# Chunk 3's second batch in natural row order, its tables built earlier, and one key load on another queue, in a fused attention and feed-forward kernel

## The chip, the cores and the metric

The kernel runs on one core of one Trainium2 chip. The metric is device time in microseconds (us) of one execution; lower is better. TensorE (PE) multiplies matrices, VectorE (DVE), ScalarE (ACT) and GpSimd (POOL) work on elements, and SyncE (SP) only issues transfers. GpSimd and ScalarE issue transfers too, each on a queue of its own.

## What is computed

Decayed linear attention in blocks of 64 rows, for 4 batches, 8 heads, 768 positions and 64 features, with a state handed from block to block, followed by a two-layer feed-forward step on all 3072 rows:

```python
Dmask = np.where(rel >= 0, lam[:, None, None] ** rel[None, :, :], 0.0)
lam_pow = lam[:, None, None] ** (pos[None, :, None] + 1)
lam_block = lam ** block
for b in range(nb):
    intra = np.einsum('bhic,bhjc->bhij', qb, kb) * Dmask[None]
    intra = np.einsum('bhij,bhjd->bhid', intra, vb)
    inter = np.einsum('bhid,bhde->bhie', qb * lam_pow[None], kv_state)
    out[:, :, sl] = intra + inter
    kb_dec = kb * rev_pow[None]
    kv_state = lam_block[None, :, None, None] * kv_state + np.einsum('bhsd,bhse->bhde', kb_dec, vb)
...
h = x @ w_in                      # x: 3072 x 512, w_in: 512 x 2048
g = np.maximum(h, 0.0) + alpha * np.minimum(h, 0.0)
return (g @ w_out).astype(np.float32)
```

## The kernel before

**Tiling.** A chunk is 512 rows: 256 positions (W) of two batches. There are six chunks, c = 0 to 5; chunk c covers positions c // 2 * 256 onward of batches 2 * (c % 2) and the next one. Within a chunk the work on attention goes in four units: batch bi (0 or 1) and half of the heads hh. Units are numbered 4c + 2 bi + hh, so units 14 and 15 are chunk 3, batch 1 (line 393).

**Two row orders.** For chunks below FIRST = 4 (line 75), a partition holds two neighbouring rows (`fetch`, lines 82 and 83), so that a load is one transfer with 512 B pieces, and the work goes in blocks of 128 positions (L). A unit then has a score matrix in pairs, two masks of 128 x 512 (`masked`, lines 617 to 627) and two states (`state`, `aged`, step L // N = 2 in `follows`). From chunk 4 on, a partition holds rows in their natural order: a load is two transfers with 256 B pieces (lines 85 and 86), the blocks have 64 positions (N), scores and outputs have half as many columns, a unit has one mask (line 642) and four states in a row, each of two scaled sums (L685). The second order has its own tables: nmask, nkdecay, nrdecay, nqdecay, built by `places_in_order` (five iotas on POOL, L320 to L322), `order_factors` (ACT, L325), `order_ahead` (DVE, L328), `order_mask_log` (two steps on POOL, L334 and L341), `order_query_log` (POOL, L346), `order_mask` (ACT, L354), `order_key_decay` (ACT, L357 and L358) and `order_query_decay` (ACT, L362).

**What happens to a unit.** k and q are loaded: k always as float32 on SyncE's queue (`load`, L100), q either so, or as float16 with the conversion in the transfer, on GpSimd's queue (`load16`, L110); v always the latter. `cast` (L398 ACT, L400 DVE, L402 POOL) makes float16 copies of what came as float32; `key_decayed` (L444, POOL) multiplies the keys by their decay; `turn` transposes k and q on TensorE (L466, L471), `turned` copies the result out of PSUM; `turn_by_dma` (L492) does the same by a transfer for units 12 and on. `decayed` (L508) makes the decayed queries. `cluster(old, new)` (L517 to L607) is the TensorE block that gives old its outputs and new its scores and state products. `out_of` copies the outputs to xT, from which the feed-forward step takes its rows.

**The feed-forward step.** `up` (L720: four products into one PSUM bank), `below` (ACT, L731), `gate` (DVE, L743), then `down` (L753: four products per part) and `store`. The bank of an up is free again when its gate has read it. bi None means both batches at once; in the first chunks it goes batch by batch.

**What sets the order.** Every engine runs its instructions in program order, and the program is written out by hand for chunks 0 and 1 and the attention of chunks 1 to 3 (lines 786 to 1175). From chunk 2 on a loop (lines 1255 to 1273) weaves the attention steps of chunk c + 1 evenly between the products of chunk c; in its first round the nine table builders are interleaved with the first nine attention steps (lines 1257 to 1269). GpSimd's queue is first in, first out: loads of w_in (`load_win`), w_out (`load_wout`), q and v as float16. `hold` (L97) writes one element of a tile early, so that the transfer into it has one thing to wait for.

Of the kernel before, what the change touches and what calls it, by code (L numbers as in the profile page):

```python
# [11 lines left out]
def kernel(  # L12
# [61 lines left out]
    N = 64  # L74
    FIRST = 4

    def fetch(queue, src, x, c, bi, part):

        h0, n = (0, H) if part is None else (part * H // 2, H // 2)
        pb, b = c // 2, 2 * (c % 2) + bi  # L80
        x, rows = x[:, ds(h0, n), :], src[b, ds(h0, n), ds(pb * W, W), :]
        if c < FIRST:
            queue.dma_start(out=x, in_=rows.rearrange("h (p e) d -> p h (e d)", e=2))  # L83
        else:
            for e in range(2):
                queue.dma_start(out=x[:, :, ts(e, D)], in_=rows[:, ts(e, L), :].rearrange("h p d -> p h d"))
# [11 lines left out]

    def load(x, c, bi, part=None):
        fetch(nc.sync, {"k": k, "q": q}[x], raw(x, c, bi), c, bi, part)  # L100

# [336 lines left out]
    def key_decayed(n, eng="G"):  # L438
        c, bi, hh = units[n]
        kr = view(raws[c, bi, "k"], hh)  # L440
        kdec = half_pool.tile([128, 2, 4, D], fp16, tag="kdec", name="kdec", bufs=4)
        for e in range(2):
            decay = kdecay[:, ds(4 * hh, 4), e] if c < FIRST else nkdecay[:, ds(4 * hh, 4)]
            engine(eng).tensor_tensor(  # L444
                out=kdec[:, e],
                in0=kr[:, e],
                in1=decay.unsqueeze(2).to_broadcast([128, 4, D]),
                op=ALU.mult,
            )
        T.setdefault(n, {})["kdec"] = kdec  # L450
# [47 lines left out]
    def decayed(n, eng="G"):  # L498
        c, bi, hh = units[n]
        t = T[n]  # L500
        qdT = qkt_pool.tile([128, 2, 2, L], fp16, tag="qdT", name="qdT")

        first = 1 if c // 2 == 0 else 0
        out, src = (
            y[:, :, :, ds(first * 64, L - first * 64)].rearrange("p e h (a j) -> p (e h) a j", j=64)
            for y in (qdT, t["qT"])
        )
        engine(eng).tensor_tensor(  # L508
            out=out,
            in0=src,  # L510
            in1=(qdecay if c < FIRST else nqdecay)[:, hh].rearrange("p e h j -> p (e h) j").unsqueeze(2).to_broadcast([128, 4, 2 - first, 64]),
            op=ALU.mult,
        )
        t["qdT"] = qdT
# [5 lines left out]
    def cluster(old, new, other=False):  # L520
# [3 lines left out]
        part = ot = acc = None  # L524
        if old is not None or units[new][0] < FIRST:
            acc = None if other else ps.tile([128, 2, 512], fp32, tag="acc", name="acc")
            part = [bank(a, "h_acc") if other else acc[:, a] for a in range(2)]
            ot = [x[:, 0:256].rearrange("p (h i) -> p h i", h=2) for x in part]
        if old is not None:
# [6 lines left out]
            def states(own):  # L536


                for e in range(1 if co < FIRST else 2):
                    for hl in range(2):  # L540
                        a = hl if own else 1 - hl
                        before = R.get((bb, ho, 4 * pbo + 2 * a if co < FIRST else 4 * pbo + 2 * e + a))
                        if before is None:
                            continue
                        for hp in range(2):
                            if co < FIRST:
# [14 lines left out]
            def outputs():  # L561
                nc.tensor.wait_ge(apart, waits[0])
                states(True)
                for hl in range(2):
                    for e in range(2):
                        for hp, a in QUADS:
                            p = ds(a * 64, 64)
                            if co < FIRST:
                                o, x = ot[a][ds(hp * 64, 64), hl, :], to["sm"][hl][p, hp, 1 - e, :]
                            else:  # L570
# [5 lines left out]
                                start=(2 * pbo + a == 0 and hl == 0 and e == 0),  # L576
                                stop=(e == 1 or co >= FIRST),
                                skip_group_check=True,
# [5 lines left out]
        if new is not None:  # L584
# [5 lines left out]
            for hp in range(2):  # L590
                for e in range(2):
                    for a, hl in QUADS:
                        p = ds(hl * 64, 64)
                        if c < FIRST:
                            o = sc[ds(a * 64, 64), hl].rearrange("p (h x e j) -> p h x e j", h=2, x=2, e=2)[:, hp, 1 - e]
# [6 lines left out]
                        )  # L602
        if old is not None and (new is None or c < FIRST):
            outputs()
        if new is not None:
            kv = t["kv"] = [
                (part[a] if c < FIRST else sc[:, a])[:, 256:512].rearrange("p (e h d) -> p e h d", e=2, h=2)  # L607
                for a in range(2)
            ]
            for hp in range(2):  # L610
                for e in range(2):
                    for hl in range(2):
                        for a in range(2):
                            if 4 * pb + 2 * e + a + 1 == S // N and c >= FIRST:
                                continue
                            p = ds(a * 64, 64)
                            nc.tensor.matmul(  # L617
                                kv[a][ds(hl * 64, 64), 0 if c < FIRST else e, hp, :],
                                lhsT=t["kdec"][p, e, hp + 2 * hl, :],
                                rhs=vn[p, e, hp + 2 * hl, :],  # L620
                                start=(c >= FIRST or old is None and hp == 0 and e == 0),
                                stop=(c >= FIRST or e == 1),
                                skip_group_check=True,
                            )
        if old is not None and not (new is None or c < FIRST):
            outputs()
# [37 lines left out]
    def follows(n, a):  # L664

        c, bi, hh = units[n]
        step = L // N if c < FIRST else 1
        b, i = 2 * (c % 2) + bi, 4 * (c // 2) + a * step
# [4 lines left out]
    def state(n, a):  # L673
# [8 lines left out]
        else:  # L682
            decay = rdecay if c < FIRST else nrdecay
            for hp in range(2):
# [76 lines left out]
    def store(c, t, c0=0, n=DM):  # L761
# [4 lines left out]
        rows = out[ds(b * S + pb * W, W), ds(c0, n)]  # L766
        rows = rows.rearrange("(j e) d -> e j d" if c < FIRST else "(e j) d -> e j d", e=2)[t // 2]
        nc.scalar.dma_start(out=rows, in_=o_sb[:, 0:n])
# [63 lines left out]
    cluster(None, 0)  # L832
    load_win(0, 256)
    mask_log(3)
# [4 lines left out]
    masked(0, 1)  # L839
    load_win(256, 256)  # L840
    fill(4)
# [46 lines left out]
    load("k", 1, 0)  # L888
    load("k", 1, 1)
    below(0, 1, 0)  # L890
# [50 lines left out]
    gate(0, 10, None)  # L941
    up(0, 12, None, 1)
    load16("v", 1, 1)
    key_decayed(4, "G")
# [8 lines left out]
    down(0, 2, 0, 0)  # L953
    load_wout(4, 4)
    turn(4)
# [112 lines left out]
    aged(12, 0)  # L1068
    aged(8, 1)
    gate(1, 1, 1)  # L1070
# [9 lines left out]
    up(1, 4, 1, 0)  # L1080
    out_of(8, "A")
    cast(11, "k", "G")
    masked(9, 0)
# [29 lines left out]
    gate(1, 6, None)  # L1113
    out_of(9, "A")
    cast(13, "q", "G")
    masked(10, 0)
# [82 lines left out]
    def in_order(x):  # L1199
        return units[x][0] >= FIRST  # L1200

# [53 lines left out]
    for c in range(2, NC):  # L1255
        att = attention_steps(c + 1) if c + 1 < NC else []
        if FIRST > 2 and c == 2:
            early = [
                places_in_order,
                order_factors,  # L1260
                order_ahead,
                lambda: order_mask_log(0),
                order_key_decay,
                lambda: order_mask_log(1),
                order_query_log,
                order_mask,
                order_query_decay,
            ]
            att = [y for z in zip(early, att) for y in z] + att[len(early) :]
        ups = [lambda f=f: up_whole(c, f) for f in range(NF)]  # L1270
# [35 lines left out]
```

## Time and profile before

| what | value |
|---|---|
| three runs | 217.02, 217.38, 218.69 us; median 217.38 |
| the profiled execution | 217.07 us; its span 215.3 |
| granted TensorE clock in it | 1.00 of full speed |
| busy: PE, weight loads, DVE, ACT, POOL | 206.1, 106.0, 123.0, 112.6, 97.4 us |
| instructions | 5683 |
| bytes | 27.28 MB read from HBM, 6.29 MB written |
| products of the feed-forward step, L720 and L753 | 96.7 and 81.2 us busy |

The span runs from the first instruction to the last; the 1.8 us around it belong to the execution but to no instruction. Busy times count instructions that compute; issuing a transfer is not counted. The page cuts the span into 40 slices and gives each engine's busy tenth in each. Below, "the chain" is the chain of work that ended last, "waits" are the idle times of an engine by what ended them, and "landing" is the moment at which a transfer's data are announced.

### The profile page before, as it was taken

How to read it: one execution, taken by the hardware profiler on the slowest of the kernel's cores; microseconds unless marked ns; L12 is line 12 of the kernel's file. 1: busy time of each engine (PE TensorE's matmuls, PEld its weight loads, DVE VectorE, ACT ScalarE, POOL GpSimd, SP SyncE). 2: the span in 40 equal slices, each digit the busy share in tenths (PEclk: the TensorE clock that was granted, in tenths of full speed). 3: DMA queues.
4: the chain of work that ended last, by engine and by line, in shares of the span. 5: the costliest groups of instructions: out<-in, count | busy, mean ns of one | idle time of the engine just before them, and what ended most of it. 6: DMA issues, size and time to landing. Idle time of an engine off the chain costs nothing.

```text
span 215.3 us, 5683 instructions
## 1 busy us (share of the span) xinstructions
PE 206.1 (96%) x2350; PEld 106.0 (49%) x2350; DVE 123.0 (57%) x259; ACT 112.6 (52%) x213; POOL 97.4 (45%) x155
## 2 busy tenths in 40 slices
PE   7978997899999999999999999999999999999993
PEld 2656543557665545454444444544444444444442
DVE  2787783849768785456576556756654344443000
ACT  5966665536656565465555555454444434443121
POOL 7899428867889561973895256422000000000000
PEclk9999999999999999999999999999999999999999
DMA  4999999999999494697689995313011101100212
GB/s 116 251 189 181 208 215 190 209 209 207 272 250 252 105 214 35 150 194 100 102 93 216 216 219 112 80 53 97 0 52 50 43 9 49 49 27 24 97 59 89
DMA packets 71194, 28.43 MB, mean 132 GB/s; under 512 B 52080, under 2 KB 68224, under 8 KB 71168
## 3 DMA queue, kind: packets, MB, share of 16 engines
q0 software_dynamic: 26592, 8.65, 35.9%
q1 hardware_dynamic: 40800, 13.11, 32.0%
q10 hardware_dynamic: 3776, 6.31, 8.1%
q8 instruction: 18, 0.29, 0.6%
q14 instruction: 8, 0.07, 0.1%
HBM read 27.28 MB, written 6.29 MB: 156 GB/s over the span
## 4 chain that ended last, share of the span: by engine, by line
PE 80%; DMA 7%; POOL 6%; ACT 3%; issue 1%; DVE 0%; ACTq 0%; POOLq 0%
PE h_ps L720 34%; PE o_ps L753 32%; DMA qh<-in_q_dram 7%; PE o_ps L775 6%; PE acc L552 3%; POOL kdec L444 2%; PE s L600 2%; PE acc L572 2%; POOL w_in_sb L116 2%; PE tp L471 1%; ACT qkT L398 1%; PE tp L466 1%; POOL qdT L508 1%; PE acc L617 1%; ACT L248 1%
## 5 line engine op out<-in xcount | busy, mean ns | idle before, releaser
L743 DVE SCALAR_TENSOR_TENSOR g<-m,oma,h_ps 128x512 f16<-128x512 f32 (+1 forms) x106 | 73.0, 696 | 64.1 <-ACT m L731 62.4
L720 PE MATMUL h_ps<-xT,w_in_sb 128*128 128x512 f16 (+1 forms) x424 | 96.7, 359 | 1.0 <-ACT R L679 0.6
L731 ACT ACTIVATE m<-h_ps 128x512 f32<-128x512 f32 (+1 forms) x106 | 59.0, 556 | 55.8 <-PE h_ps L720 53.9
L753 PE MATMUL o_ps<-w_out_sb,g 128*128 128x512 f16 x320 | 81.2, 379 | 0.0
L720 PEld LDWEIGHTS <-w_in_sb 128*128 128x128 f16 x424 | 39.6, 98 | 41.6 <-DMA w_in_sb<-in_moe_w_in_dram 1.1
L753 PEld LDWEIGHTS <-g 128*128 128x128 f16 x320 | 30.9, 98 | 35.8
L764 ACT ACTIVATE o_sb<-o_ps 128x512 f32<-128x512 f32 (+2 forms) x25 | 14.5, 579 | 18.8 <-PE o_ps L775 11.0
L444 POOL TENSOR_TENSOR kdec<-kraw,kdecay 128x256 f16<-128x256 f32 x32 | 19.5, 633 | 7.4 <-DMA kraw<-in_k_dram 6.6
L633 DVE TENSOR_TENSOR sm<-s,dmask 128x512 f16<-128x512 f32 x32 | 21.2, 684 | 2.8 <-PE s L600 2.7
L398 ACT ACTIVATE xT<-acc 128x512 f16<-128x512 f32 x22 | 13.1, 597 | 13.3 <-PE acc L572 9.0
L508 POOL TENSOR_TENSOR qdT<-qkT,nqdecay 128x512 f16<-128x512 f16 x8 | 9.3, 1164 | 18.9 <-DMA qkT<-qk 8.7
L701 POOL TENSOR_TENSOR old<-R,rdecay 128x128 f32<-128x128 f16 x21 | 8.3, 410 | 17.4 <-DVE R L681 14.8
L775 PE MATMUL o_ps<-w_out_sb,g 128*128 128x512 f16 (+2 forms) x80 | 14.0, 336 | 0.0
L508 POOL TENSOR_TENSOR qdT<-qkT,qdecay 128x512 f16<-128x512 f16 (+1 forms) x11 | 11.3, 1029 | 3.0 <-DVE qkT L400 1.9
L552 PE MATMUL acc<-qdT,R 64*64 64x64 f16 (+1 forms) x216 | 10.9, 217 | 0.2
L775 PEld LDWEIGHTS <-g 128*128 128x128 f16 x80 | 7.2, 98 | 6.9
L685 DVE SCALAR_TENSOR_TENSOR R<-R,nrdecay,s 128x64 f16<-128x64 f16 x48 | 10.5, 275 | 0.0
L552 PEld LDWEIGHTS <-R 64*64 64x64 f16 x224 | 5.9, 104 | 8.8 <-issue 5.9
L444 POOL TENSOR_TENSOR kdec<-kraw,nkdecay 128x256 f16<-128x256 f32 x16 | 9.5, 613 | 0.0
L572 PE MATMUL acc<-sm,vh 64*64 64x128 f16 (+1 forms) x352 | 8.5, 209 | 0.0
L83 POOL DMA_DIRECT2D vh<-in_v_dram x8 | 7.6, 945 | 0.8 <-POOLq L1290 0.8
L398 ACT ACTIVATE qk<-qraw 128x512 f16<-128x512 f32 x11 | 6.9, 624 | 2.0 <-DMA qraw<-in_q_dram 1.1
(107 smaller groups left out, 152.3 us busy)
## 6 DMA issues: line engine op xcount, KB each, us to landing
out_dram<-o_sb ACTq DMA_DIRECT2D x23, 256.0 KB, 2.3
kraw<-in_k_dram SPq DMA_DIRECT2D x12, 256.0 KB, 5.1
kraw<-in_k_dram SPq DMA_DIRECT2D x6, 512.0 KB, 11.4
qraw<-in_q_dram SPq DMA_DIRECT2D x10, 256.0 KB, 6.9
vh<-in_v_dram POOLq DMA_DIRECT2D x8, 256.0 KB, 10.5
w_out_sb<-in_moe_w_out_dram POOLq DMA_DIRECT2D x4, 512.0 KB, 9.4
w_in_sb<-in_moe_w_in_dram POOLq DMA_DIRECT2D x3, 512.0 KB, 6.7
qh<-in_q_dram POOLq DMA_DIRECT2D x5, 256.0 KB, 11.1
```

What stands on the lines that cost most here:

```text
L398: nc.scalar.activation(out, in_, AF.Copy)
L444: engine(eng).tensor_tensor(out=kdec[:, e], in0=kr[:, e], in1=decay.unsqueeze(2).to_broadcast([128, 4, D]), op=ALU.mult,)
L508: engine(eng).tensor_tensor(out=out, in0=src, in1=(qdecay if c < FIRST else nqdecay)[:, hh].rearrange("p e h j -> p (e h) j").unsqueeze(2) ...
L552: nc.tensor.matmul(o, lhsT=before[ds(hl * 64, 64), hp, :], rhs=x, start=not own and e == 0, stop=False, skip_group_check=True,)
L572: nc.tensor.matmul(o, lhsT=vo[p, e, hp + 2 * hl, :], rhs=x, start=(2 * pbo + a == 0 and hl == 0 and e == 0), stop=(e == 1 or co >= FIRST), ...
L633: nc.vector.tensor_tensor(out=t["sm"][hl], in0=t["s"][:, hl].rearrange("p (h x j) -> p h x j", h=2, x=2), in1=mask_of(hl, hh), op=ALU.mult,)
L720: nc.tensor.matmul(h_ps[:, 0:n] if bi is None else h_ps[:, 0:n].rearrange("p (e j) -> p e j", e=2), lhsT=w_in_sb[:, gi, ts(f, 128)], rhs=x ...
L731: nc.scalar.activation(m[:, 0:n], HP[c, f, bi][:, 0:n], AF.Relu, scale=-1.0)
L743: nc.vector.scalar_tensor_tensor(out=g, in0=mv, scalar=oma[:, f : f + 1], in1=hv, op0=ALU.mult, op1=ALU.add)
L753: nc.tensor.matmul(O[c, t], lhsT=G[c, f][:, t // 2, t % 2, :], rhs=w_out_sb[:, f, :], start=(f == 0), stop=(f == NF - 1),)
L764: nc.scalar.activation(o_sb[:, 0:n], o_ps[:, 0:n], AF.Copy)
L775: nc.tensor.matmul(o_ps[:, 0:n], lhsT=G[c, f][:, t // 2, t % 2, :], rhs=w_out_sb[:, f, ds(c0, n)], start=(f == 0), stop=(f == NF - 1),)
```

## The change

FIRST becomes a pair, (3, 1), and every test on the chunk becomes a test on (chunk, batch). So chunk 3, batch 1, units 14 and 15, goes over to the natural row order, with its loads, decays, clusters, masks, states and stores. Its tables are built earlier, between instructions of chunks 0 and 1. The second batch's keys of chunk 1 move from SyncE's queue to GpSimd's. w_in's first two loads have 128 and 384 columns instead of 256 and 256. Some calls change places.

```diff
-    FIRST = 4
+    FIRST = (3, 1)
...
-        if c < FIRST:
+        if (c, bi) < FIRST:
             queue.dma_start(out=x, in_=rows.rearrange("h (p e) d -> p h (e d)", e=2))
...
-    def load(x, c, bi, part=None):
-        fetch(nc.sync, {"k": k, "q": q}[x], raw(x, c, bi), c, bi, part)
+    def load(x, c, bi, part=None, queue=nc.sync):
+        fetch(queue, {"k": k, "q": q}[x], raw(x, c, bi), c, bi, part)
...
-    slopes(2)
     key_decay()
     turn(0)
     decay_mask(0)
     cast(1, "k", "V")
+    slopes(2)
     query_log()
...
-    load_win(0, 256)
+    load_win(0, 128)
...
-    load_win(256, 256)
+    load_win(128, 384)
...
     load("k", 1, 0)
-    load("k", 1, 1)
...
     aged(11, 0)
+    places_in_order()
     up(0, 5, None, 0)
...
     load16("v", 1, 0)
+    load("k", 1, 1, None, nc.gpsimd)
     gate(0, 5, None)
     up(0, 7, None, 2)
     below(0, 6, None)
+    order_factors()
     gate(0, 6, None)
+    order_ahead()
...
     gate(0, 7, None)
+    order_mask_log(0)
     gate(0, 8, None)
+    order_mask_log(1)
     up(0, 10, None, 2)
     below(0, 9, None)
     load16("q", 1, 1)
+    order_query_log()
...
     up(0, 12, None, 1)
+    load_wout(4, 4)
     load16("v", 1, 1)
     key_decayed(4, "G")
...
     down(0, 2, 0, 0)
-    load_wout(4, 4)
     turn(4)
...
     gate(1, 1, 0)
+    up(1, 2, 0, 1)
     down(0, 0, 3, 2)
     out_of(6, "A")
+    order_key_decay()
     masked(7, 0)
     state(7, 0)
-    up(1, 2, 0, 1)
...
     turn(8)
-    cast(9, "k", "V")
...
     turned(8, "V")
+    cast(9, "k", "V")
...
     aged(12, 0)
-    aged(8, 1)
...
     out_of(8, "A")
+    order_mask()
...
     out_of(9, "A")
+    order_query_decay()
...
     def in_order(x):
-        return units[x][0] >= FIRST
+        return units[x][:2] >= FIRST
...
-        if FIRST > 2 and c == 2:
-            early = [
-                places_in_order,
...
-            ]
-            att = [y for z in zip(early, att) for y in z] + att[len(early) :]
```

The other tests on FIRST, in `key_decayed`, `decayed`, `cluster`, `follows`, `state` and `store`, change in the same way.

More of the change, by code (lines that the diff above doesn't have):

```diff
@@ L510, in decayed @@
             in0=src,
[L511 removed]
+            in1=(qdecay if (c, bi) < FIRST else nqdecay)[:, hh].rearrange("p e h j -> p (e h) j").unsqueeze(2).to_broadcast([128, 4, 2 - first, 64]),
             op=ALU.mult,
@@ L524, in cluster @@
         part = ot = acc = None
-        if old is not None or units[new][0] < FIRST:
+        if old is not None or units[new][:2] < FIRST:
             acc = None if other else ps.tile([128, 2, 512], fp32, tag="acc", name="acc")
@@ L536, in states @@
             def states(own):
-                for e in range(1 if co < FIRST else 2):
+                for e in range(1 if (co, bo) < FIRST else 2):
                     for hl in range(2):
                         a = hl if own else 1 - hl
-                        before = R.get((bb, ho, 4 * pbo + 2 * a if co < FIRST else 4 * pbo + 2 * e + a))
+                        before = R.get((bb, ho, 4 * pbo + 2 * a if (co, bo) < FIRST else 4 * pbo + 2 * e + a))
                         if before is None:
@@ L602, in cluster @@
                         )
-        if old is not None and (new is None or c < FIRST):
+        if old is not None and (new is None or (c, bi) < FIRST):
             outputs()
@@ L606, in cluster @@
             kv = t["kv"] = [
-                (part[a] if c < FIRST else sc[:, a])[:, 256:512].rearrange("p (e h d) -> p e h d", e=2, h=2)
+                (part[a] if (c, bi) < FIRST else sc[:, a])[:, 256:512].rearrange("p (e h d) -> p e h d", e=2, h=2)
                 for a in range(2)
@@ L613, in cluster @@
                         for a in range(2):
-                            if 4 * pb + 2 * e + a + 1 == S // N and c >= FIRST:
+                            if 4 * pb + 2 * e + a + 1 == S // N and (c, bi) >= FIRST:
                                 continue
@@ L617, in cluster @@
                             nc.tensor.matmul(
-                                kv[a][ds(hl * 64, 64), 0 if c < FIRST else e, hp, :],
+                                kv[a][ds(hl * 64, 64), 0 if (c, bi) < FIRST else e, hp, :],
                                 lhsT=t["kdec"][p, e, hp + 2 * hl, :],
                                 rhs=vn[p, e, hp + 2 * hl, :],
-                                start=(c >= FIRST or old is None and hp == 0 and e == 0),
-                                stop=(c >= FIRST or e == 1),
+                                start=((c, bi) >= FIRST or old is None and hp == 0 and e == 0),
+                                stop=((c, bi) >= FIRST or e == 1),
                                 skip_group_check=True,
                             )
-        if old is not None and not (new is None or c < FIRST):
+        if old is not None and not (new is None or (c, bi) < FIRST):
             outputs()
@@ L766, in store @@
         rows = out[ds(b * S + pb * W, W), ds(c0, n)]
-        rows = rows.rearrange("(j e) d -> e j d" if c < FIRST else "(e j) d -> e j d", e=2)[t // 2]
+        rows = rows.rearrange("(j e) d -> e j d" if (c, t % 2) < FIRST else "(e j) d -> e j d", e=2)[t // 2]
         nc.scalar.dma_start(out=rows, in_=o_sb[:, 0:n])
```

22 lines of the change are left out of this document (7 added, 15 removed).

## The prediction, made before the changed kernel was run

> **What bounds the kernel now.** I read the slices of the page first, then the chain that ended last, then the waits and the timeline around its one transfer.
>
> ```profile
> PE   7978997899999999999999999999999999999993
> DMA  4999999999999494697689995313011101100212
> ```
>
> Each digit is the busy tenth of 5.4 us. TensorE (PE) is full from slice 8 (43 us) to the end; the transfers are full from slice 1 to slice 12 (5 to 70 us). So a microsecond can be won only where PE still stands idle, in the first 45 us, or by giving PE less to do.
>
> ```profile
> 30.00:35.00 5.00, 3.76 (x28) 1.84 (x27) 2.25 (x4) 2.24 (x4) 4.04 (x6) 1.00 1.52 202
> 35.00:40.00 5.00, 4.25 (x117) 2.81 (x116) 3.90 (x9) 4.38 (x8) 4.16 (x7) 1.00 1.50 196
> 40.00:45.00 5.00, 4.94 (x81) 2.63 (x79) 2.88 (x6) 1.92 (x5) 4.46 (x7) 1.00 1.22 210
> 45.00:50.00 5.00, 5.00 (x77) 2.91 (x76) 3.63 (x10) 2.13 (x5) 2.38 (x6) 1.00 1.53 200
> ```
>
> Stretch, length, then busy us of PE, weight loads, DVE, ACT, POOL, the granted clock and DMA. PE is idle for 1.24 us in 30 to 35, 0.75 in 35 to 40, nothing after 45. The same table gives 2.3 us idle in 5 to 20 us and 0.17 in 20 to 30. What ends the 1.24:
>
> ```profile
> 19.14 14.73 DMA qh<-in_q_dram
> 33.92 0.43 PE tp L471 x8
> 34.37 1.03 ACT qkT L398
> 35.45 0.38 PE tp L466 x4
> 35.83 0.36 PE tp L471 x8
> 36.22 0.54 ACT qkT L398
> 37.41 0.53 ACT k L398
> ...
> PE tp L471 <- DMA qh<-in_q_dram: 1.2, 1, 1.2
> POOL kdec L444 <- DMA kraw<-in_k_dram: 6.6, 1, 6.6
> ```
>
> The first seven are the chain (start, length, what), the last two the waits. The q of chunk 1, batch 0, call it q10 (I name k11, v10 and so on alike: tensor, chunk, batch), is issued at 19.14 and lands 14.73 us later; TensorE's transposes (L471) wait for it until 33.92, the 1.24 us. After that the chain is a ping-pong of PE transposes and ACT copies. Why q10 is so late is in the transfers, 30 to 32 us and then 34 to 36:
>
> ```profile
> q1 hardware_dynamic: 547, 0.28, 69.0%
> q0 software_dynamic: 548, 0.14, 67.6%
> ...
> q0 software_dynamic: 1424, 0.36, 180.9%
> q1 hardware_dynamic: 5, 0.00, 0.6%
> ```
>
> Packets, MB written, share. While SyncE's queue (q1) carries k11, GpSimd's (q0) gets 274 packets a us, one for one; alone it gets 712. k11 is not needed before its cast at 37.3 (L398), and holds up q10, which is.
>
> **k11 on GpSimd's queue, behind v10.** Landings here are an issue's start plus its time to landing, from the view of transfers in a short window. By the trace's packet records k10 ends on q1 at 29.6, q10 has then some 390 of its 1024 packets, and the other 634 took until 32.0 beside k11. Alone they take 634/712 = 0.9 us: the last at 30.5, landing (1.84 later, as now) at 32.35. PE reaches the waiting transposes when the ones before end, 32.68 (32.29 + 0.39). So the wait of 1.24 us goes. Ends: 0 saved if q0 goes on at 274, 1.24 if at 712; I take 1.2, since the rate alone is measured two us later on the same rows. Late next is the ping-pong above, whose lengths stay: 0.75 us of idleness is moved, not removed. k11 itself, behind v10 (1.45 us alone), ends near 33.6 and lands near 35.1 (34.63 now); its readers, the ACT cast at 37.30 and POOL's at 37.25, come 1.2 us earlier, 36.1, so about 1 us is left. No row shows this load on q0: at 274 a us it would land near 37.2 and cost 1.1.
>
> **POOL, 21 to 35 us.** POOL idles 6.55 us there, waiting for k10 until 30.71. Added: five iotas (0.84 us from 74.91 to 75.75), the k11 issue (0.94, the row of v loads with as many packets), the two mask products (1.04 and 1.28), the query product (0.62), and a w_out issue (0.79) moved up: 5.5 us in all. The first product waits for ACT's factors, which come after below(0,6), 26.2. In order: iotas to 22.4, v10 23.3, k11 24.2, products 26.5 to 28.8, q11 29.7, query product 30.3, w_out 31.1, v11 32.0, then kdec of units 4 and 5, 32.0 to 34.4 instead of 30.71 to 33.23. PE wants the first at 36.35 - 1.2 = 35.1: 1.9 us spare. Without that cover each us of POOL is one of PE. Queued behind the waiting product are q11 (issued 29 instead of 22.4, but q0 is busy until 33.6 anyway; landing near 36.5, wanted 38.31 - 1.2 = 37.1), w_out (near 39, wanted 40.2) and v11 (near 40.5, wanted 43). Cost 0; upper end 1 us.
>
> **ACT and DVE beside it.** ACT has 0.27 us idle per block of 0.86, the factors (0.30) fill it. DVE's gates run 0.75 in 0.86 with the bank free 0.25 before its next use; order_ahead (0.19) fits barely: 0.05 (0 to 0.2). order_key_decay (0.29 + 0.19, now near 47) delays state(7,0), then aged(7,1) on POOL and kdec(8), needed 2 us later: 0. order_mask (0.62) and order_query_decay (2 x 0.41, near 65) stand ahead of a below; gate and bank have 0.2 to 0.7: 0.1 (0 to 0.6). aged(8,1) gone: POOL 0.4 less, DVE two scaled sums (2 x 0.28) for one (0.28): 0. slopes later: the oma row (0.18) moves between cast and copy of unit 0, up to 0.3 us there, but the chain in 7 to 19 us is POOL's: 0.05.
>
> up(1,2,0) goes ahead of the last part of down(0,0), which reads w_out that landed at 47.12 for 48.01: the same PE work in another order, 0, and 0.4 us more time for that load. cast(9) goes behind the copy of unit 8: DVE order only, 0 (turn 9 at 53.24 has 0.9 to spare).
>
> **w_in as 128 + 384.** The same bytes and issues (0.80 each). First up at 16.65: its weights landed at 16.36 and its xT left ACT at 16.42, so one wait hides the other: 0 (bounds 0 to 0.64). The second part, wanted at 18.00, lands as now near 17.34.
>
> **Units 14 and 15 in order.** A cluster between two products on PE:
>
> ```profile
> 100.08 0.25 PE L552 MATMUL acc<-qdT,R 64*64 64x128 f16 x4
> 100.17 0.39 PE L600 MATMUL s<-qkT 64*64 64x128 f16 x16
> 100.41 0.25 PE L552 MATMUL acc<-qdT,R 64*64 64x128 f16 x4
> 100.49 0.39 PE L572 MATMUL acc<-sm,vh 64*64 64x128 f16 x16
> 100.71 0.29 PE L617 MATMUL acc<-vh,kdec 64*64 64x64 f16 x16
> 100.94 1.04 PE L753 MATMUL o_ps<-w_out_sb,g 128*128 128x512 f16 x4
> ```
>
> It takes 0.86 us here (100.08 to 100.94). In order, at 111.37 to 112.03, it takes 0.66; with an old unit in pairs and a new one in order, 105.36 on, 0.73. The three clusters 13-14, 14-15, 15-16 cost 0.86 + 0.86 + 0.73 = 2.45 and then 0.73 + 0.66 + 0.66 = 2.05: 0.4 us less (0.3 to 0.5). DVE gets 0.9 us more per unit (eight sums of 0.275 and one mask of 0.69 for two masks and two sums of 0.29) in stretches where it is busy 6 of 10 us: 0. Its k, q and v come in twice the packets, on SyncE's and GpSimd's queues: 0 here, the second rival below. The tables leave the loop of chunk 2, where PE is never idle: 0.
>
> **Sum.** -1.2 - 0.4 + 0.2 = -1.4 us. The profiled execution took 217.07 us (span 215.3, 1.8 around it); the median of the runs is 217.38. 217.38 - 1.4 = 216.0.
>
> **Rivals.** (a) The gain is caught later. PE 1.2 us ahead meets loads of chunk 2 that still come when the saturated transfers bring them: q21 landed at 53.09 for transposes at 53.57, 0.48 spare; w_out's last part 47.12 for 48.01. If landings stay, 0.5 of the 1.2 is kept: 216.7. Against it: their issues move up with the program, and 0.6 us of transfer time is saved by not alternating. (b) Slower: the in-order k31 and q31 hold back the transfer that turns unit 12. That transpose is issued on SyncE behind q31 at 66.09, lands 69.86, and PE wants it at 72.16, or 71.1 with the gain. 256 B packets alone ran at 1938 in 76 to 78 us, 0.25 MB/us, the 512 B ones at 645 in 63.5 to 64.5, 0.33: 1 MB takes 4.2 us for 3.2, landing at 70.9, just in time: no loss. But chunk 4's first k and q, beside v, took from 73.21 to 83.07; less 2.3 for the start (the page's output stores), 7.6 us, where k31 and q31 take 3.65 now (64.84, the landing before them, to 68.49): 3.9 more, landing 73.8, 2.7 us of stall, 218.7. It decides from a landing at 72.5, which eats the whole 1.4. The Trainium skill, "DMA: Bandwidth & Descriptors", section Specifications, asks for at least 512 B a transfer for line rate, and says shorter ones do a read-modify-write; it speaks for (b). The trace agrees in direction: a quarter less at 256 B. (c) The head shortens too: if the weights and not xT ended the wait at 16.65, the earlier 128 columns save its 0.64 as well: 215.4, or 215.1 with costs at nothing.
>
> **Chances.** Forecast 0.50 (its own range 215.2 to 216.8), (a) 0.20, (b) 0.15, (c) 0.15. About 1% is what a measurement of this kernel can tell from no change, 2.2 us: faster needs 215.2. That takes most of (c) and the low edge of the forecast, 0.18; slower needs 219.6, the bad half of (b) and a late k11 and q11 together with (a), 0.14; within, 0.68. The range leaves out the far ends of (b) and (c): 214.8 to 218.4.
>
> **What would show it.** Right: no PE wait on q10, q10 landing by 32.7, PE reaching each product of chunk 1 about 1.2 us earlier; three clusters of 0.73, 0.66, 0.66. Wrong: POOL's kdec of unit 4 after 35, ACT's cast of unit 6 or the turn of unit 6 waiting for k11 or q11, or any PE wait between 45 and 75 us, where there is none now. (b) shows as PE waiting on a qkT transfer near 71.

## The result, and the profile after

The kernel before ran at a median of 217.84 us in 20 runs (216.96 to 219.33), the changed one at 216.63 us in 20 runs (215.67 to 218.42). The ratio is 0.9935, with a 95% interval of 0.9915 to 0.9955: 0.65% less, so within 1%, and 0.6 us above the forecast of 216.0 us. As a difference, which leaves out that the kernel before now has the higher median, the forecast was -1.4 us and the medians give -1.21. The profiled execution took 215.67 us (span 213.9), 1.40 us less than the one before. Two of the profiles below, those of e4_ahead_early and e7_up_back, caught executions some 3 us longer than the others of the same kernel, and only durations and waits of single instructions are read from them.

The slices of the page of the changed kernel:

```profile
PE   7979999999999999999999999999999999999994
DMA  4999999999999799998899973313011001101212
```

TensorE is now full from slice 3 on (counted from 0, as in the prediction); before, slices 3, 6 and 7 stood at 8, 7 and 8. The table by stretches of the changed kernel (stretch, length, busy us of PE, weight loads, DVE, ACT and POOL, granted clock, DMA):

```profile
30.00:35.00 5.00, 4.85 (x41) 2.47 (x39) 2.98 (x5) 3.27 (x5) 4.99 (x8) 1.00 1.58 234
35.00:40.00 5.00, 4.40 (x121) 2.94 (x116) 4.56 (x10) 3.89 (x7) 4.97 (x9) 1.00 1.47 198
45.00:50.00 5.00, 4.84 (x80) 3.19 (x78) 2.62 (x8) 2.30 (x7) 1.97 (x4) 1.00 1.56 200
50.00:55.00 5.00, 4.83 (x97) 3.57 (x94) 4.02 (x9) 3.61 (x8) 4.78 (x7) 1.00 1.48 242
70.00:75.00 5.00, 4.82 (x75) 2.44 (x74) 4.21 (x9) 2.95 (x5) 3.39 (x6) 1.00 0.65 148
```

From 30 to 35 us PE idles 0.15 us in place of 1.24. But after 45 us, where it had no idle time, it now lacks 0.16, 0.17 and 0.18 us in the last three stretches. POOL, which idled there, is full from 30 to 40 us. PE's waits in the changed kernel (us in total, times, longest):

```profile
PE h_ps L720 <- DVE g L743: 0.3, 2, 0.2
...
PE s L600 <- DMA qkT<-qk: 0.2, 1, 0.2
```

The wait on q10 is no longer in the list. Two small waits on gates (near 47 and 50.5 us) and one on the transfer that turns unit 12 (at 71.7; call it T12) are new. The queues of the changed kernel from 30 to 32 us (packets, MB, share):

```profile
q0 software_dynamic: 1304, 0.33, 171.8%
q1 hardware_dynamic: 50, 0.02, 5.6%
```

With k11 off SyncE's queue (q1), GpSimd's (q0) moves 652 packets a us, where it had 274; from 31 us on, when k10's last packets are through, 701. q10 lands at 32.69 us.

**A ledger.** For each profile I took the start of the same TensorE products as in before, both counted from the kernel's own product that starts at 20.5 us in before. The column "head" is how much later that product itself starts than in before, which differs between executions of one kernel. Minus is earlier; all in us.

| kernel | 28.8 | 46.7 | 57.0 | 75.6 | 145.3 | 211.5 | head | last landing to end |
|---|---|---|---|---|---|---|---|---|
| before | 0 | 0 | 0 | 0 | 0 | 0 | 0 | 1.57 |
| changed | +0.29 | -1.03 | -0.74 | -0.50 | -0.83 | -0.84 | -0.03 | 1.06 |
| e8_changed_again | +0.29 | -0.77 | -0.49 | +0.20 | -0.13 | -0.14 | +0.01 | 1.08 |
| e1_only_k11 | 0 | -0.38 | +0.03 | +0.53 | +0.53 | +0.53 | +1.33 | 1.64 |
| e2_k11_back | +0.29 | +0.18 | +0.46 | +0.55 | +0.23 | +0.23 | -0.13 | 1.00 |
| e3_pairs | +0.29 | -0.78 | -0.49 | -0.50 | -0.50 | -0.50 | +0.35 | 1.62 |
| e5_k11_late_sync | 0 | +0.50 | +0.50 | +0.50 | +0.51 | +0.51 | +0.01 | 1.18 |
| e6_ahead_q31 | 0 | +0.03 | +0.32 | +1.67 | +1.34 | +1.34 | +0.07 | 1.06 |
| f1_up_back_again | +0.29 | -0.73 | -0.88 | -0.89 | -1.22 | -1.23 | -0.01 | 1.06 |
| f2_up_ahead | 0 | -0.62 | -0.39 | -0.21 | -0.55 | -0.55 | +0.16 | 1.06 |
| f3_up_ahead_q31pool | 0 | -1.11 | -1.17 | +0.19 | -0.13 | -0.13 | -0.02 | 1.26 |
| f4_before_two_more_issues | 0 | +1.41 | +1.25 | +1.29 | +1.29 | +1.29 | -0.01 | 1.01 |

The second row is the change in one line: 0.29 lost by 28.8 us; 1.32 won from there to 46.7; 0.29 lost by 57; 0.24 lost by 75.6; 0.33 won in the loop of chunk 2; and 0.51 won behind the last product. With the head's 0.03 this gives 0.84 + 0.03 + 0.51 = 1.38 of the span's 1.37.

Each row is one execution, and not every step of it belongs to the edit. Three steps repeat to 0.01 or 0.02 us in every kernel of the table that has the same part of the change: the 0.29 by 28.8 us (five kernels with `order_ahead` late), the 0.28 to 0.29 from 46.7 to 57 (five with up(1,2,0) early) and the 0.32 to 0.34 from 75.6 to 145.3 (seven with units 14 and 15 in order; without, 0.01 at most). The other steps don't. f4 runs the program of the kernel before until it loads k31, at 56.2 us, and still stands at +1.41 at 46.7: TensorE waited 0.90 us for w_out's first part and 1.58 for q10. The changed kernel's two rows are 0.70 apart at the end. So a difference of less than about 1.4 us by 46.7, or 0.7 by 75.6, is read from a wait or a landing and not from the table alone.

### The profile page after: what moved, and what is told of

The parts are those of the page before. It is cut to its first block, busy times and chain, and to the rows that moved or that the text cites. A ratio compares the mean times of both kernels' runs of the same rounds, so it can differ in the third digit from the quotient of the medians.

```text
span 213.9 us, 5729 instructions
## 1 busy us (share of the span) xinstructions
PE 206.3 (96%) x2366; PEld 106.1 (50%) x2366; DVE 125.6 (59%) x270; ACT 112.5 (53%) x213; POOL 97.7 (46%) x152
## 3 DMA queue, kind: packets, MB, share of 16 engines
HBM read 27.28 MB, written 6.29 MB: 157 GB/s over the span
## 4 chain that ended last, share of the span: by engine, by line
PE 75%; DMA 13%; ACT 4%; DVE 3%; issue 1%; SPq 1%; POOL 1%; ACTq 0%; DVEq 0%
PE h_ps L720 33%; PE o_ps L753 28%; DMA kraw<-in_k_dram 6%; PE o_ps L775 6%; DMA qraw<-in_q_dram 3%; DMA qkT<-qk 2%; PE acc L552 2%; PE s L600 1%; DMA out_dram<-o_sb 1%; DVE g L743 1%; ACT qkT L398 1%; PE acc L572 1%; SPq L83 1%; PE tp L471 1%; PE tp L466 1%
## 5 line engine op out<-in xcount | busy, mean ns | idle before, releaser
L508 POOL TENSOR_TENSOR qdT<-qkT,nqdecay 128x512 f16<-128x512 f16 x10 | 11.7, 1165 | 29.5 <-PE o_ps L753 9.2
L633 DVE TENSOR_TENSOR sm<-s,dmask 128x512 f16<-128x512 f32 x28 | 18.6, 682 | 2.5 <-PE s L600 2.5
L444 POOL TENSOR_TENSOR kdec<-kraw,kdecay 128x256 f16<-128x256 f32 x28 | 17.2, 638 | 1.0 <-ACT kdecay L295 0.6
L685 DVE SCALAR_TENSOR_TENSOR R<-R,nrdecay,s 128x64 f16<-128x64 f16 x64 | 13.9, 274 | 0.0
L444 POOL TENSOR_TENSOR kdec<-kraw,nkdecay 128x256 f16<-128x256 f32 x20 | 11.9, 612 | 0.4 <-DMA kraw<-in_k_dram 0.4
L701 POOL TENSOR_TENSOR old<-R,rdecay 128x128 f32<-128x128 f16 x16 | 6.3, 408 | 8.7 <-DVE R L681 5.7
L508 POOL TENSOR_TENSOR qdT<-qkT,qdecay 128x512 f16<-128x512 f16 (+1 forms) x9 | 9.1, 1008 | 2.0 <-DMA qkT<-qk 1.5
L86 POOL DMA_DIRECT2D vh<-in_v_dram x10 | 9.1, 913 | 0.0
L384 PE MATMUL op_fill<-filler 128*128 128x512 f16 x17 | 6.8, 541 | 1.8 <-DVE sel L203 1.1
```

The costliest lines, as they stand in the source:

```text
L444: engine(eng).tensor_tensor(out=kdec[:, e], in0=kr[:, e], in1=decay.unsqueeze(2).to_broadcast([128, 4, D]), op=ALU.mult,)
L508: engine(eng).tensor_tensor(out=out, in0=src, in1=(qdecay if (c, bi) < FIRST else nqdecay)[:, hh].rearrange("p e h j -> p (e h) j").unsque ...
L633: nc.vector.tensor_tensor(out=t["sm"][hl], in0=t["s"][:, hl].rearrange("p (h x j) -> p h x j", h=2, x=2), in1=mask_of(hl, hh), op=ALU.mult,)
L685: nc.vector.scalar_tensor_tensor(out=then[:, hp, :], in0=before[:, hp, :], scalar=decay[:, 2 * hh + hp : 2 * hh + hp + 1], in1=T[n]["kv"][ ...
```

## The experiments

My theory: q10 is late because k11's transfer alternates with it, so that taking k11 away from that time wins the wait; the clusters of units 14 and 15 win 0.3 more; `order_ahead`, the earlier up(1,2,0) and T12 give back some 0.8. The rivals: the queue that k11 stands in is what matters, not the time; the gain of q10 is caught by later loads; the 256 B packets of units 14 and 15 make T12 late. The kernels named e1 to e4 shared a chip and its runs of the kernel before, then e5 to e8, then f1 to f4.

**Only k11 moved.** The kernel before, with one load moved:

```diff
     load("k", 1, 0)
-    load("k", 1, 1)
...
     load16("v", 1, 0)
+    load("k", 1, 1, None, nc.gpsimd)
```

> The kernel before with one edit: k11 issued on GpSimd's queue behind v10 instead of on SyncE's. Theory (two queues are served packet for packet, so k11 halves the rate of q10): q10 lands near 32.6 us instead of 33.87, the 1.24 us wait of TensorE on it goes, products near 45 us start 1.1 to 1.3 us earlier, and 0.8 to 1.3 us are left at the last product. Rival (the gain of the change comes from its other parts, the tables and the order of w_out and v11): q10 lands where it did, within 0.2 us, and nothing moves.

Measured: 218.10 us against 218.12, ratio 0.9993 (0.9962 to 1.0025). The wait on q10 is gone, and the time is the same. TensorE's timeline in this kernel (start, length, what, and in brackets the idle time ahead and what ended it):

```profile
35.21 1.02 PE L720 MATMUL h_ps<-xT,w_in_sb 128*128 128x512 f16 x4 [0.52 <-DVE g L743]
37.70 1.02 PE L720 MATMUL h_ps<-xT,w_in_sb 128*128 128x512 f16 x4 [0.43 <-DVE g L743]
49.54 1.02 PE L753 MATMUL o_ps<-w_out_sb,g 128*128 128x512 f16 x4 [0.51 <-DMA w_out_sb<-in_moe_w_out_dram]
74.14 0.42 PE L600 MATMUL s<-qkT 64*64 64x128 f16 x16 [0.45 <-DMA qkT<-qk]
```

Other waits stand in its place. k10 landed at 33.24 in this execution, its cast on ACT came late, and with it two gates (k10 took 12.3 us from its issue here, and 12.3 and 12.4 in e2 and f4, where k11 is not moved, so that is no work of this edit); then w_out's last part (the one due at 48.01 before) and T12 arrive after PE. The lead of 0.38 at 46.7 us is a loss of 0.53 at the end. By the medians a wait of 1.24 us was worth nothing by itself; the interval reaches from 0.8 us less to 0.5 us more, and the profile is of an execution 0.9 us above this kernel's median. This is rival (a), and in this profile it took more than the 0.7 us that I gave it.

**k11 back on SyncE, the rest of the change kept.**

```diff
     load("k", 1, 0)
+    load("k", 1, 1)
...
-    load("k", 1, 1, None, nc.gpsimd)
```

> The changed kernel with k11 back on SyncE's queue, all else kept. Theory: q10 lands near 33.8 again, TensorE waits about 1 us for it, and the last product starts 0.7 to 1.2 us later than in the changed kernel, about as in the kernel before. Rival: the rest of the change carries the gain, q10 stays near 32.7 and the last product moves by under 0.3 us.

Measured: 217.72 us, 0.9967 (0.9937 to 0.9997). q10 lands at 33.92 and the wait is back, in PE's waits of this kernel:

```profile
PE tp L471 <- DMA qh<-in_q_dram: 1.0, 1, 1.0
```

At 46.7 us, ahead of anything that T12 does, this kernel is 1.21 us behind the changed one and 0.95 behind e8. At the end it is 1.07 behind the one (+0.23 against -0.84) and 0.37 behind the other. By the medians it is 0.7 us (ratios 0.9967 and 0.9935, whose intervals overlap). So within the whole change the move of k11 is worth about its wait up to 46.7 us, and at the end as much of it as the later loads leave. Alone it was worth nothing that can be seen. What fits that is the issue of w_out's second part ahead of v11, which the whole change has and e1 has not: that part landed between 38.98 and 40.47 us in eight profiles with it (those of e4 and e7 left out), and between 40.96 and 42.42 in the four without, e1's among them (42.20). This one move was not run by itself.

**Units 14 and 15 in pairs, everything else of the change kept.**

```diff
-    FIRST = (3, 1)
+    FIRST = (4, 0)
```

> The changed kernel with units 14 and 15 back in pairs of rows (the boundary at chunk 4), tables still built early. Theory (natural order gives TensorE 0.33 to 0.4 us less in three clusters, and its loads cost 0.2 us of waiting for the transposing transfer of unit 12): the transposing transfer lands about 1.5 us earlier, no wait near 71 us, clusters 0.86, 0.86, 0.73, and the last product 0.1 to 0.3 us later than in the changed kernel. Rival (the doubled packets cost more than the clusters save): the last product is earlier than in the changed kernel.

Measured: 217.03 us, 0.9953 (0.9924 to 0.9982). Two things follow. From 75.6 us to the end this kernel wins nothing (-0.50 and -0.50), the changed one 0.34 (-0.50 to -0.84): that is what the clusters are worth. And T12 lands at 71.73, as late as in the changed kernel (71.71), though k31 and q31 come in 512 B pieces here. That doesn't clear the smaller packets, because T12's input was later here: q30 landed at 65.29 in place of 64.43, and the cast of it ended at 66.51 in place of 65.65. SyncE's timeline shows what the natural order does (the first line is from the kernel before, the others from the changed one):

```profile
58.67 3.58 SPq L83 DMA_DIRECT2D qraw<-in_q_dram  x1
...
61.49 5.22 SPq L86 DMA_DIRECT2D qraw<-in_q_dram  x2
66.88 4.84 SPq L492 DMA_TRANSPOSE qkT<-qk  x2
```

q31's two issues in natural order keep SyncE until 66.71, and T12 is issued 1.23 us behind the end of its input's cast; in e3, as in before, it is issued 0.03 us behind it. Counted from the end of that cast, T12 lands 5.74 to 7.04 us later in the five profiles with q31 in natural order ahead of it on SyncE's queue (changed, e2, e8, f1, f2; mean 6.29) and 3.80 to 6.04 in the five with pairs (before, e1, e3, e5, f4; mean 5.07). So the natural order seems to cost T12 some 1.2 us, though the two ranges overlap. In e3 PE didn't wait, because it came there some 0.6 us later (by the ledger and the head, 0.14 us ahead of before, where the changed kernel was 0.77 ahead). The clusters, on the timeline of the changed kernel, 14 to 15:

```profile
95.13 0.26 PE L552 MATMUL acc<-qdT,R 64*64 64x64 f16 x8
95.22 0.30 PE L600 MATMUL s<-qkT 64*64 64x64 f16 x16
95.34 0.30 PE L617 MATMUL s<-vh,kdec 64*64 64x64 f16 x16
95.47 0.26 PE L552 MATMUL acc<-qdT,R 64*64 64x64 f16 x8
95.55 0.34 PE L572 MATMUL acc<-sm,vh 64*64 64x64 f16 x16
95.83 1.04 PE L720 MATMUL h_ps<-xT,w_in_sb 128*128 128x512 f16 x4
```

95.13 to 95.83 is 0.70 us. 13 to 14 takes 0.74 and 15 to 16 takes 0.66, together 2.10; in this experiment 0.85, 0.85 and 0.73, together 2.43.

**order_ahead before GpSimd's product.** In the changed kernel:

```diff
     gate(0, 4, None)
+    order_ahead()
     load16("v", 1, 0)
...
-    order_ahead()
```

> The changed kernel with order_ahead moved up behind gate(0,4), a stretch in which GpSimd has nothing to run. Theory (the 0.68 us of order_ahead at 26.85 us came from running beside GpSimd's product on nmask): it takes about 0.2 us, the gates keep their pace, the products near 28 us start 0.26 to 0.29 us earlier, and of that 0.1 to 0.3 us are left behind the arrival of q10. Rival (the operation takes 0.6 us wherever it stands among the gates): it takes 0.6 us and only its place moves.

Measured: 216.51 us, 0.994 (0.9909 to 0.9971): no gain that can be seen. The place itself is clear. On the timeline of the changed kernel:

```profile
26.44 1.04 POOL L334 TENSOR_TENSOR nmask<-places,loglam 128x512 f32<-128x512 f32 x1 [2.25 <-ACT places L325]
26.85 0.68 DVE L328 TENSOR_SCALAR ahead<-places_i 128x64 f32<-128x64 int32 x1
27.67 1.27 POOL L341 TENSOR_TENSOR nmask<-nmask,ahead 128x512 f32<-128x512 f32 x1 [0.19 <-DVE ahead L328]
```

DVE's small operation starts within GpSimd's product (26.44 to 27.48) and ends at 27.53, 0.05 us behind it: 0.68 us. Moved ahead of the product it took 0.19 us, and with it went the 0.29 us lost at 28.8 (column 28.8 of e6 and f2, where the same move was made). What becomes of the 0.29 us later is read from f2, below. The Trainium skill, "SBUF — State Buffer", section "SBUF: two separate sides", says that GpSimd and some of DVE's operations share a pair of ports, which the one that starts first holds for its whole instruction while the other is blocked; the end of L328 so close behind the product agrees. That L328 is one of the operations that take this pair, no run here shows.

**k11 on SyncE, but later.** The kernel before, with the load held until the turn of gate(0,7), issued at 27.88:

```diff
-    hold("k", 1, 1)
...
     load("k", 1, 0)
-    load("k", 1, 1)
...
     gate(0, 7, None)
+    hold("k", 1, 1)
+    load("k", 1, 1)
```

> The kernel before with one edit: k11 stays on SyncE's queue, but is held back until gate(0,7), about 27.8 us, so that its packets come behind q10's. Theory (what held q10 up was that k11's packets ran at the same time, not whose queue they were on): q10 lands near 32.6 us and TensorE's wait on it is under 0.2 us, as with k11 on GpSimd's queue. Rival (taking it to GpSimd's queue matters in itself): q10 lands near 33.8. In both, k11 may land after 36.1 us and cost its readers up to 0.5 us, so the time moves by less than the wait.

Measured: 217.30 us against 217.62, 0.9982 (0.9949 to 1.0014). q10 lands 2.07 us behind w_out's first part (3.64 in before, 2.43 in the changed kernel, 1.88 in e1), and PE doesn't wait for it. So q10 is freed by the time at which k11 comes, not by its queue. What else came late, on PE's timeline:

```profile
31.16 1.90 PE L753 MATMUL o_ps<-w_out_sb,g 128*128 128x512 f16 x8 [0.43 <-DMA w_out_sb<-in_moe_w_out_dram]
36.43 0.32 PE L617 MATMUL acc<-vh,kdec 64*64 64x64 f16 x16 [0.60 <-DMA vh<-in_v_dram]
41.89 1.02 PE L753 MATMUL o_ps<-w_out_sb,g 128*128 128x512 f16 x4 [0.68 <-DMA w_out_sb<-in_moe_w_out_dram]
```

The three waits are 1.71 us together, but not all of that is the load's doing. w_out's first part landed at 31.11, 0.88 us later than in before, while k11's packets ran from 32 to 36 us: the first wait belongs to this execution, as the 0.90 in f4 does, and the same lateness is in v10 (0.87) and in w_out's second part (0.88). What k11 does is to run beside v10 now, packet for packet as it did beside q10, so that v10 lands 3.21 us behind q10 in place of 1.65. None of the three waits stands in the changed kernel's list, where k11 follows v10 on GpSimd's queue. That this order of landings keeps the gain there is argued, not shown: w_out's first part was 0.85 us earlier in that profile.

**q31 behind T12.** In the changed kernel, with order_ahead early as in e4:

```diff
-    load("q", 3, 1)
...
     turn_by_dma(13)
+    load("q", 3, 1)
```

> The changed kernel with order_ahead behind gate(0,4), and the load of q31 issued behind the transposing transfers of units 12 and 13 instead of ahead of them. Theory (the lead won near 33 us is cut at 71 us by the transfer that turns unit 12, which stands behind q31 in SyncE's queue): it lands 1.5 to 2.5 us earlier, near 69.5, no wait of TensorE near 71 us, and the last product is 0.3 to 0.6 us earlier against the head of its own run than in the changed kernel, about 0.2% of the time. Rival (q31's lateness then stops GpSimd at its cast and costs it back): GpSimd waits at the cast of unit 14's q and the last product is not earlier.

Measured: 217.44 us, 0.9981 (0.9958 to 1.0005). T12 lands at 70.48 and nothing waits for it, but q31 lands at 75.25. The timeline of this kernel:

```profile
75.37 0.61 POOL L402 CAST qk<-qraw 128x512 f16<-128x512 f32 x1 [3.25 <-DMA qraw<-in_q_dram]
...
76.37 0.29 DVE L681 TENSOR_TENSOR R<-acc,old 128x128 f16<-128x128 f32 x1 [1.27 <-POOL old L701]
...
77.38 1.46 PE L720 MATMUL h_ps<-xT,w_in_sb 128*128 128x512 f16 x6 [1.29 <-DVE g L743]
```

POOL's cast waits for q31, behind it on POOL stands the aging of a state, DVE waits for that 1.27 us and with it the gates, and PE then waits 1.29 us for a bank. So T12's landing can be had, but q31 has no 4 us to give. This kernel's loss of 1.67 by 75.6 in the ledger also holds a wait of 1.16 us for w_out's first part, which landed at 31.92 there, 1.66 later than in the changed kernel's profile.

**up(1,2,0) back behind the state of unit 7, twice.** In the changed kernel:

```diff
-    up(1, 2, 0, 1)
     down(0, 0, 3, 2)
...
     state(7, 0)
+    up(1, 2, 0, 1)
```

> The changed kernel with up(1,2,0) behind down's last part again, as in the kernel before. Theory (with up(1,2,0) ahead, TensorE waits 0.16 and 0.17 us for gates; without it, it would wait 0.2 to 0.4 us for w_out's last part, which landed at 47.21): the waits on gates near 47 and 50 us go, one on w_out comes, and the last product moves by under 0.2 us. Rival: no wait on w_out, and the last product is 0.3 us earlier.

Measured: 215.82 us, 0.9918 (0.9890 to 0.9946). The waits on gates near 47 and 50.5 are gone, and PE doesn't wait for w_out. The changed kernel itself was run beside it:

> The changed kernel itself, on the same chip as these, to compare them with. All theories: ratio to the kernel before 0.991 to 0.996; against the head of its own run TensorE is about 1.0 us earlier at 37 us, 0.7 at 60 and 0.8 at the last product.

Measured: 216.51 us, 0.9937 (0.9912 to 0.9961). Here, too, PE waits for T12, and longer, on this kernel's timeline:

```profile
72.49 0.42 PE L600 MATMUL s<-qkT 64*64 64x128 f16 x16 [0.64 <-DMA qkT<-qk]
```

And once more on another chip, the edit of e7 in more rounds:

> The changed kernel with up(1,2,0) behind down's last part, once more and in more rounds, for a profile that can be set beside the changed kernel's. Theory (the swap costs two waits on gates, 0.3 us, and saves none): no wait on a gate near 47 and 50 us, none on w_out, ratio to the kernel before 0.990 to 0.994, 0.1 to 0.2% under the changed kernel's 0.9935. Rival (the earlier 0.9918 was chance): ratio 0.9935 or more, and a wait on w_out where the profile has one.

Measured: 216.30 us, 0.9911 (0.9878 to 0.9943), its profiled span 213.5. In the ledger the changed kernel loses 0.29 from 46.7 to 57 us, and 0.28 in e8; f1 wins 0.15 there (as f4 does, so 0.15 of that is not the edit's). T12 landed at 71.31, PE didn't wait. The ratios of e7 and f1 lie 0.002 below the changed kernel's two (0.9935 and 0.9937), some 0.4 us; the intervals overlap, so it is the ledger and the vanished waits that decide for this order, and its size stays at 0.3 to 0.4. With f2, below, it has the lowest ratio of all, 0.9% under the kernel before.

**Both of these moves.** f1 with order_ahead ahead of v10's load, as in e4.

> The same with order_ahead behind gate(0,4) as well. Theory (order_ahead beside GpSimd's product costs 0.29 us near 28 us): 0.2 us, no loss near 28 us, up to 0.3 us less than f1 at the last product where no transfer takes it back. Rival (whoever comes earlier to 71 us waits there for the transfer that turns unit 12): the same as f1 within 0.1 us, and a longer wait at 71.

Measured: 216.26 us, 0.9913 (0.9881 to 0.9944), the same as f1. L328 took 0.19 us and column 28.8 is 0; but PE came 0.52 us too early for w_out's first part (landed at 31.36) and 0.32 too early for its last (47.90). In this profile what is won at 28.8 us is taken back where the next load is due; w_out's first part was 0.74 us later in it than in f1's.

**q31 on GpSimd's queue.** f2 with one more edit:

```diff
-    load("q", 3, 1)
+    load("q", 3, 1, None, nc.gpsimd)
```

> The same as f2 with q31 on GpSimd's queue behind v31, so that the transfer that turns unit 12 stands behind k31 alone on SyncE's queue. Theory (its place behind q31 is what makes it late): it lands near 70 or earlier, no wait of TensorE at 71, another 0.2 to 0.6 us. Rival (the 16 engines are shared, so q31 on the other queue runs beside it and delays it as much; and its two issues cost GpSimd 1.8 us in a full stretch): no gain, or a loss of up to 0.5 us at the gates.

Measured: 217.57 us, 0.9975 (0.9945 to 1.0006). T12 is issued at 66.08 and lands 6.3 us later, at 72.41: PE waits 0.86 us. T12 is issued 0.03 us behind its input's cast here, and still lands 6.36 behind it, as in the kernels where SyncE issues it late. So it isn't SyncE's issuing alone that makes T12 late, and off SyncE's queue q31 gains nothing. The time is also 0.6% above f2's, of which a wait of 0.86 us would be the larger part. The Trainium skill, "DMA: Bandwidth & Descriptors", section "Issuing engines are not separate DMA queues", says that transfers from all engines end up on the same 16 engines and interleave; the 6.3 us agree, against 4.02 in e6, where q31 wasn't under way; the 3.77 of before, where it was, don't.

**Two more issues on SyncE in the kernel before.** The changed kernel ends 1.06 us behind the landing of its last store, the one before 1.57. To see whether the number of SyncE's instructions does that, k31 and q31 were loaded in two halves each:

```diff
-    load("k", 3, 1)
+    load("k", 3, 1, 0)
+    load("k", 3, 1, 1)
...
-    load("q", 3, 1)
+    load("q", 3, 1, 0)
+    load("q", 3, 1, 1)
```

> The kernel before with k31 and q31 each loaded by two issues, one for each half of the heads: the same packets, two instructions more on SyncE. It is about the end: from the last landing to the end of the span 1.57 us passed in the kernel before and 1.06 in the changed one, the difference in one gap of 0.45 us between two of SyncE's last waits. Theory (the gap depends on how many instructions SyncE has run): 1.0 to 1.2 us here. Rival (it belongs to another part of the change): 1.5 to 1.7.

Measured, in one run of 217.76 us: 1.01 us from the last landing to the end. The loads changed nothing at the end but the count.

## Why the prediction was right, and where it was not

**The wait on q10** was right in place, cause and size. Forecast: landing at 32.35 and 1.2 us; measured: landing at 32.69, no wait, and 1.32 us won between 28.8 and 46.7 (1.06 and 1.02 in e8 and f1, where k10 came late). The rate was taken at 712 packets a us and was 701 once k10 was through. PE's wait was 1.03 (e2), 1.24 (before) and 1.58 us (f4) with k11 issued at once on SyncE, and there was none in the other kernels. e2 shows that it hangs on k11, e5 that it hangs on k11's time.

**The later catch**, rival (a), was a thing apart from the sum in the prediction, and is a part of it: e1 shows the whole gain caught, and the changed kernel loses 0.24 us of it from 57 to 75.6 (0.18 of that its wait for T12), e8 0.69 (0.64).

**T12.** The prediction had 70.9, "just in time", or 73.8 by rival (b). It landed at 71.71 and 72.45 (e8), and PE waited 0.18 and 0.64 us: the sign that was named for (b), at a small part of its 2.7 us. The term that failed is the 3.77 us from issue to landing (66.09 to 69.86), taken from the one profile of before. With q31 ahead of it in pairs, too, T12 took 5.10 to 6.01 us in four other profiles (e1, e3, e5, f4): the row was the shortest of all. The 1.0 us for the smaller packets is near the 1.2 by which the means differ (e3), and the 3.9 of (b) shows nowhere. What the prediction left out is that q31's two issues keep SyncE until T12's input has been ready for 1.23 us. T12 caps what an earlier PE can keep: in the changed kernel whatever PE wins before 71 us beyond 71.7 is lost there.

**order_ahead** was mis-sized: 0.05, at most 0.2, forecast from a duration of 0.19; measured 0.29, since the operation took 0.68 beside GpSimd's product. The prediction put GpSimd's new products and DVE's new operation into the same two microseconds and costed each from a row where it stood alone.

**up(1,2,0)**, "the same PE work in another order, 0", failed as well, and put waits between 45 and 75 us, which the prediction had named as a sign of being wrong: 0.3 to 0.4 us (e7, f1). Ahead of the last down it wants its bank about 1 us earlier (the length of that down part), and the gate that frees it hasn't got earlier: waits of 0.16 and 0.17 us stand on it and on up(1,4,0), the next up in the same bank.

**The clusters** were right: 2.10 us in place of the forecast 2.05, 0.34 won in the ledger where 0.4 was forecast.

**w_in and the tables** were right at nothing. The first weights land at 14.62, 1.74 earlier, and the first up starts at 16.51 in place of 16.65; by 20.5 us 0.03 is left, so (c) is out. On POOL kdec of unit 4 starts at 32.10 (forecast 32.0), k11 lands at 35.65 (35.1), q11 at 36.73 (36.5), and nothing waits for them.

**The end** was not in the prediction: 0.51 us. With it the sum is -1.32 + 0.29 + 0.29 + 0.24 - 0.34 - 0.51 = -1.35, and -0.03 of the head: -1.38 for the forecast -1.4. The agreement is partly luck: 0.82 us of costs stood where 0.2 was forecast, and the end, which has nothing to do with the change's meaning, paid 0.51 of it. The pair of profiles is luck, too: the other profile of the changed kernel, e8, took 216.42 us, 0.65 less than the one before and not 1.40.

**What stays open.** Why k10 takes 10.9 us from issue to landing in before, 11.5 in the changed kernel and 12.2 to 12.3 in e8, f1 and e1, on the same issue. Why T12 took only 3.77 us in the profile of before, and how much of its lateness in the changed kernel is q31's issues and how much its packets. And whether L328's 0.68 us is the ports or something else that the two engines share.

## What to carry to other kernels

Where transfers are full, a wait on one of them is taken away by moving in time what alternates with it, and the gain is only kept as far as the next loads have slack: list them with their landings, and take an issue-to-landing time from more than one execution before calling it "just in time". Cost a small operation that is put beside another engine's long one at the length that such an operation has there, not at its length alone. Putting the same products in another order is free only if the banks they write are free earlier too.

## What the runs showed of the hardware

**When q10 lands.** With k11 issued at once on SyncE, q10 lands 3.64, 3.64 and 3.70 us behind w_out's first part (before, e2, f4); in the other eleven profiles 1.50 to 2.54.

**A stop in SyncE's program at a fixed count.** SyncE has 87 recorded instructions in before, 88 in e1 and e3, 90 in the changed kernel. In before, e1 and e3 its 79th is the wait for the last store, and the 80th comes 0.47 to 0.48 us later; elsewhere such waits follow each other in 0.06 to 0.09. In e5 and f3 the 79th stands one wait earlier, and the 80th again comes 0.47 to 0.48 us later, but the last store lands in that time, so it costs nothing. In the other nine the 79th lies further ahead, among waits 3.4 us apart that would hide such a stop. The time from the last landing to the end is 1.57 to 1.64 us in the first three and 1.00 to 1.26 in all others. In all 14 profiles one packet of 8 KB on a queue of kind "instruction" (q14) starts 1.08 to 1.09 us behind the end of the 79th, wherever that lies. So this is a place in SyncE's program at which instructions are brought in; that this is what stops SyncE is likely, but not shown.

**Issuing a load keeps SyncE.** q31 took 3.58 us of it in one issue of 512 B pieces (before), 3.41 in two issues of such pieces (f4), and 5.22, 4.75 and 5.00 in two issues of 256 B pieces (changed, e8, f1).

**One kernel's executions differ by 2 us** (217.84 median, 216.96 to 219.33 in before) at a granted clock of 1.00. In the profiles, those of e4 and e7 left out, the head starts up to 1.3 us later, and w_out's first part lands between 29.9 and 31.9 us, so that a wait of half a us on a load appears in one execution and not in the next.
